# A transformer block's backward pass: attention output gradients turned in four pieces a chunk, chunk 0's q, k and v gradients kept in SBUF, a new order and new homes

## The chip, the core and the metric

The kernel runs on one core of one Trainium2 chip. The core has a matrix engine (TensorE, PE in the profile), a vector engine (VectorE, DVE), an activation engine (ScalarE, ACT), GpSimd (POOL) and a synchronisation engine (SyncE, SP), which here does nothing but issue transfers. All five run their own instruction streams in order; a transfer, once issued, is carried by 16 DMA engines. The metric is the device time of one execution in microseconds. Before the change three runs took 540.76, 541.15 and 544.3 us, median 541.15.

## What is computed

A pre-norm transformer block, forward and backward in one program, in bf16: S = 2048 rows, D = 512 columns, 32 heads of 16, F = 1792. The reference, cut to what matters:

```
q, k, v = (layernorm(x) @ wqkv) split into 32 heads of 16
idx  = pos[:, None] - 2 * arange(8)[None, :]         # window of 8 keys, 2 apart
attn = softmax(where(idx >= 0, q . k[idx] / 4, -1e9))
h    = x + (sum over the window of attn * v[idx]) @ wo
y    = h + gelu(layernorm(h) @ w1 + b1) @ w2 + b2
out, vjp = jax.vjp(block, x, wqkv, wo, w1, b1, w2, b2)
return (out, *vjp(grad_out))
```

Eight tensors come out: y and the gradients of x, wqkv, wo, w1, b1, w2 and b2.

## The kernel before, in words

The 2048 rows are worked in four chunks of 512 rows (CH). The Python functions do not issue instructions; each calls `op` (L84) to record an operation: its engine, the buffers that it reads and writes, and a function that issues its instructions. At the end `emit` (L118) walks ORDER, a table of operation numbers at the end of the file, and issues them in just that sequence. It is one sequence for all engines, so each engine's own program is what falls to it. HOMES, a second table, gives each buffer its address in SBUF (units of 64 bytes) or its PSUM bank. Two buffers may share a place if one is dead by ORDER before the other is first used, so a home can add a wait. Waits themselves are set by the framework from the buffers and addresses.

Transfers go through helpers, so in the profile they carry the helper's line: `load` L268, `store` L273, `xload` (a transfer that transposes 2-byte elements on its way) L277, `gather` L507. Nearly all are on SP's queue, where an instruction that waits holds up all that stand behind it.

The stages of a chunk, with the names that the profile uses:

- Layer norm of x (L355 to L402, tile `ln`), turned to column-major `ln1T`, for chunk 0 by TensorE (L445), for the others by a transposing transfer. Key, query and value projections (L674 with weights `wk` and `wq`, L699 with `wv`), evicted to `kt`, `qt` and `tmv` by ScalarE. While the first x is loaded, TensorE runs matmuls on a zeroed tile `wz` (L304).
- Attention scores: VectorE multiplies queries with shifted keys (`prf`, L517, 2.29 us each, four to a chunk), TensorE sums the products over a head's 16 elements (L525). Softmax, the weighted sum of values (gathered as `Ro`, `prbo` L557, L566), the output projection (L790), the residual and the second layer norm.
- Feed-forward: L826 (h times w1), gelu pieces on ScalarE (L828 `xb`, L831 `gl`), L880 (times w2, result `h2s` at L882). Feed-forward backward: L908, L910, L922, layer-norm backward L604 to L617 with results `ghr`, turned to `ghT`.
- `p3_go` (L930): the gradient of the attention's output, `got`, by L946 (`ghT` times `woT`), evicted by ScalarE in two halves. It is column-major, and the value-gradient step needs it row-major in DRAM (`go_d`), since `gather` reads bands of rows from there. `tm_dma` (L469) does that: a transposing transfer into the tile `tmgod`, then a store to `go_d`.
- `p3_dots` (L952): VectorE's products `prb` of `got` and the shifted values `vw` (L517 again), sums, softmax backward. `p3_bands` (L991): gradients of q, v and k, from gathered bands of DRAM rows (`Rq` from `k_d`, `Rv` from `go_d`, `Rk` from `q_d`), products on VectorE (`prbq`, `prbv`, `prbk`, L557), sums on TensorE (L566), evicted by ScalarE to `gqs`, `gvs` and `gks` (L571). `p3_gl1` (L1017) turns these by transposing transfers (`gqkvT`), multiplies with wqkv (L1042), and ends in layer-norm backward and the gradient of x (`gx`).
- Weight gradients, `wg_ffn` (L1083), matmuls at L1068 in groups, placed by ORDER wherever TensorE would otherwise wait, from about 200 us to the end. The last are those of wqkv, from `gqs`, `gvs`, `gks` and the layer-norm output `ln1b`.

Since the wqkv gradients come last and need all four chunks, chunk 0's `gqs`, `gvs` and `gks` are stored to DRAM (`gq_d`, `gv_d`, `gk_d`) in the kernel before and loaded again as `gq3in`; how many chunks are treated so is KEEP (L1012, L1122 to L1130). Before, KEEP is 1. `tm_dma` has two forms, chosen by `off`, the offset in the source tile, which for `got` is 0: one transposing transfer for the whole chunk, and a store whose pieces are 128 elements (256 bytes) long.

Of the kernel before, what the change touches and what calls it, by code (L numbers as in the profile page):

```python
# [148 lines left out]
def kernel(  # L149
# [319 lines left out]
    def tm_dma(fm, off, dst, c, back, tag, pm):  # L469
# [3 lines left out]
        if off:  # L473
# [609 lines left out]
    def wg_ffn():  # L1083
# [37 lines left out]
        for sel in (0, 2, 1):  # L1121
            G_ = sb("gq3in", [P, KEEP, 4, D]) if KEEP else None  # L1122
            for c in range(KEEP):
# [16 lines left out]
    for i in (1, 0, 2):  # L1140
        b = wv if i == 2 else wqk[i]
        load(b, lambda b=b: b(), lambda i=i: A_wqkv[:, i * D:(i + 1) * D].rearrange("(a p) j -> p a j", p=P), 512,
             tag="wqkv", q="ACT" if i in WQA else "SP")
# [112 lines left out]
KEEP = 1  # L1256
# [9 lines left out]
TMD = (('go', 0), ('go', 1), ('go', 2), ('go', 3))  # L1266
LNK = 0
# [179 lines left out]
```

## Time and profile before

| what | value |
|---|---|
| runs shown | 540.76, 541.15, 544.3 us |
| the profiled execution | 541.34 us, its span 539.6 us |
| TensorE busy | 524.6 us (97% of the span), 3023 matmuls |
| VectorE, ScalarE, GpSimd busy | 476.6, 335.6, 15.6 us |
| transfers | 136.61 MB, mean 253 GB/s |
| HBM | read 54.73 MB, written 37.84 MB |

The span is what the hardware profiler saw of the program; the reported time has 1.74 us around it. "Busy" counts the time that an engine executes; matmuls are pipelined, so their shown durations (379 ns) overlap, and a long run of them starts one every 0.22 us. In a row of the timeline the columns are the start, the length, the engine, the source line, the operation, what it writes and reads, the count, and in brackets the idle time before it with what ended it. "SPq" is SP's queue: the time that an issue held it, which includes waits for earlier instructions; the landing of a transfer comes later and is listed apart.

### The profile page before, as it was taken

The page shows a single profiled execution, that of the slowest core. Times are in us where ns is not written, and L with a number is a line of the kernel's source. Part 1 is how long each engine was busy: PE and PEld are TensorE (multiplying, and loading weights), DVE is VectorE, ACT ScalarE, POOL GpSimd, SP SyncE. Part 2 cuts the span into 40 slices and gives each one's busy share as a digit, 9 for nine tenths or more (in the row PEclk, how much of TensorE's full clock was granted, in tenths as well). Part 3 has the DMA queues.
Part 4 walks back from the last instruction along what each step waited for, and adds up shares of the span by engine and source line. Part 5 has one row for each costly group of instructions (what it writes and reads, how often), then busy time and mean ns, then how long its engine had stood idle before and what let it go on. Part 6 is the DMA issues. An engine that isn't in the chain of part 4 may idle for free.

```text
span 539.6 us, 8072 instructions
## 1 busy us (share of the span) xinstructions
PE 524.6 (97%) x3023; PEld 233.1 (43%) x3023; DVE 476.6 (88%) x607; ACT 335.6 (62%) x586; POOL 15.6 (3%) x23
## 2 busy tenths in 40 slices
PE   7899999999999999999999999999999999999997
PEld 3343444444444444444444444446444343443443
DVE  6889999999989999899741658999999999999993
ACT  6867859999999968977303623124343465252773
POOL 0110200000001000000000000000000000000003
PEclk9999999999999999999999999999999999999999
DMA  6999897988999999988999999999999999999977
GB/s 205 184 336 285 287 297 234 231 260 252 190 236 275 270 251 244 265 224 170 193 216 209 211 228 196 218 276 206 308 324 322 279 324 252 317 315 278 321 216 225
DMA packets 230871, 136.61 MB, mean 253 GB/s; under 512 B 188400, under 2 KB 218800, under 8 KB 226736
## 3 DMA queue, kind: packets, MB, share of 16 engines
q1 hardware_dynamic: 230448, 135.06, 98.1%
q0 software_dynamic: 384, 1.05, 0.7%
q8 instruction: 23, 0.38, 0.3%
q14 instruction: 16, 0.13, 0.1%
HBM read 54.73 MB, written 37.84 MB: 172 GB/s over the span
## 4 chain that ended last, share of the span: by engine, by line
PE 67%; DVE 14%; DMA 8%; ACT 4%; issue 3%; SPq 2%; POOL 1%; DVEq 0%; ACTq 0%
PE ps L1068 21%; PE ps L826 8%; PE ps L908 7%; PE ps L922 7%; PE ps L1042 7%; PE ps L880 6%; PE ps L566 3%; DMA Rk<-q_d 3%; DVE prf L517 3%; DVE prbk L557 3%; PE ps L946 3%; SPq L268 2%; PE ps L525 2%; DMA gqkvT<-gvs 2%; DMA v_d<-tmv 1%
## 5 line engine op out<-in xcount | busy, mean ns | idle before, releaser
L908 PE MATMUL ps<-goT,w2T 128*128 128x512 bf16 x224 | 54.1, 379 | 0.9 <-DVE h2s L882 0.8
L880 PE MATMUL ps<-w,gl 128*128 128x512 bf16 x224 | 51.3, 379 | 0.4 <-ACT gl L831 0.4
L826 PE MATMUL ps<-ln2T,w 128*128 128x512 bf16 x224 | 51.2, 379 | 0.2 <-ACT e L747 0.2
L922 PE MATMUL ps<-w1T,xb 128*128 128x512 bf16 x224 | 50.8, 379 | 0.0
L604 ACT ACTIVATE gyr<-ps,rstd 128x512 bf16<-128x512 f32 x28 | 19.0, 680 | 46.5 <-PE ps L922 31.4
L1042 PE MATMUL ps<-wqkvT,gqkvT 128*128 128x512 bf16 x192 | 44.5, 380 | 0.7 <-DMA gqkvT<-gvs 0.7
L283 ACT CAST wgs<-ps 128x512 bf16<-128x512 f32 (+1 forms) x30 | 16.4, 557 | 45.0 <-PE ps L1068 42.6
L910 DVE SCALAR_TENSOR_TENSOR xb<-xb,ps 128x512 bf16<-128x512 bf16 x56 | 37.0, 682 | 7.7 <-PE ps L908 7.4
L828 ACT ACTIVATE xb<-ps,b1c 128x512 bf16<-128x512 f32 x56 | 35.7, 693 | 7.8 <-PE ps L826 5.2
L1068 PE MATMUL ps<-gw1in,ln 128*128 128x512 bf16 (+1 forms) x192 | 39.5, 353 | 0.0
L1068 PE MATMUL ps<-gor,gw2in 128*128 128x512 bf16 x168 | 39.4, 379 | 0.0
L517 DVE TENSOR_TENSOR prf<-qt,kt 128x4096 bf16<-128x4096 bf16 x16 | 36.0, 2287 | 1.4 <-ACT qt L283 1.4
L557 DVE TENSOR_TENSOR prbv<-Rv,cfv 128x4096 bf16<-128x4096 bf16 x16 | 35.9, 2287 | 1.3 <-DMA Rv<-go_d 1.3
L557 DVE TENSOR_TENSOR prbq<-Rq,cfq 128x4096 bf16<-128x4096 bf16 x16 | 35.9, 2285 | 0.7 <-issue 0.5
L557 DVE TENSOR_TENSOR prbo<-Ro,cfo 128x4096 bf16<-128x4096 bf16 x16 | 35.8, 2287 | 0.7 <-PE ps L566 0.6
L517 DVE TENSOR_TENSOR prb<-got,vw 128x4096 bf16<-128x4096 bf16 x16 | 36.0, 2285 | 0.2
L557 DVE TENSOR_TENSOR prbk<-Rk,cfk 128x4096 bf16<-128x4096 bf16 x16 | 35.7, 2283 | 0.1
L1068 PEld LDWEIGHTS <-ln 128*128 128x128 bf16 x256 | 24.5, 98 | 25.1 <-issue 3.0
L908 PEld LDWEIGHTS <-w2T 128*128 128x128 bf16 x224 | 21.8, 98 | 27.9 <-issue 1.9
L880 PEld LDWEIGHTS <-gl 128*128 128x128 bf16 x224 | 21.5, 98 | 27.5 <-issue 1.3
L826 PEld LDWEIGHTS <-w 128*128 128x128 bf16 x224 | 21.6, 98 | 27.2 <-issue 1.8
L922 PEld LDWEIGHTS <-xb 128*128 128x128 bf16 x224 | 21.9, 98 | 26.5
(160 smaller groups left out, 921.0 us busy)
## 6 DMA issues: line engine op xcount, KB each, us to landing
Ro<-v_d SPq DMA_DIRECT2D x4, 1280.0 KB, 5.9
Rq<-k_d SPq DMA_DIRECT2D x4, 1280.0 KB, 7.6
Rv<-go_d SPq DMA_DIRECT2D x4, 1280.0 KB, 8.1
Rk<-q_d SPq DMA_DIRECT2D x4, 1280.0 KB, 7.7
g_d<-gl SPq DMA_DIRECT2D x9, 512.0 KB, 5.2
gh_d<-xb SPq DMA_DIRECT2D x9, 512.0 KB, 3.7
Ro<-v_d SPq DMA_DIRECT2D x4, 1024.0 KB, 7.8
Rq<-k_d SPq DMA_DIRECT2D x4, 1024.0 KB, 9.6
```

The source lines that it names most:

```text
L283: fn = lambda: A.copy(out=ap(), in_=pap())
L517: op("DVE", tt_us(4096), lambda g=g, pr=pr: V.tensor_tensor(out=pr(), in0=ql()[:, g, :].unsqueeze(1).to_broadcast([P, W, 512]), in1=_sub(k ...
L557: V.tensor_tensor(out=pr().rearrange("p j a (d h) -> p (j a) d h", h=H), in0=_sub(R()[:, o0, 0:1], [[1024, 4], [st, 2], [1, 512]]), in1=_s ...
L604: op("ACT", act_us(D, 1, True), lambda: A.activation(out=gyr()[:, j, :], in_=ps(), func=ACT.Copy, scale=rs[:, t:t + 1], accum_out=sg_[:, i ...
L826: T.matmul(ps(), lhsT=w1()[:, dc, f * P:(f + 1) * P], rhs=cols(ln2T[c], dc, c in FM2), start=(dc == 0), stop=(dc == DC - 1))
L828: op("ACT", act_us(512, 1), lambda f=f, ps=ps, xb=xb, f0=f0: A.activation(out=xb()[:, f - f0, :], in_=ps(), func=ACT.Identity, bias=b1c[:, ...
L880: T.matmul(ps(), lhsT=d["g"][f // 4]()[:, f % 4, j * P:(j + 1) * P], rhs=w2()[:, f, :], start=(f == 0), stop=(f == FT - 1))
L908: T.matmul(ps(), lhsT=w2T()[:, dc, f * P:(f + 1) * P], rhs=cols(goT, dc, True), start=(dc == 0), stop=(dc == DC - 1))
L910: op("DVE", 0.61, lambda f=f, ps=ps, z=z, f0=f0: V.scalar_tensor_tensor(out=z()[:, f - f0, :], in0=z()[:, f - f0, :], scalar=1.0, in1=ps() ...
L922: T.matmul(ps(), lhsT=d["d"][f // 4]()[:, f % 4, j * P:(j + 1) * P], rhs=w1T()[:, f, :], start=(f == 0), stop=(f == FT - 1))
L1042: T.matmul(ps(), lhsT=gT()[:, j, b * P:(b + 1) * P], rhs=wqkvT()[:, k0 + b, :], start=(i == 0 and b == 0), stop=(i == 2 and b == 3))
L1068: T.matmul(ps()[:, 0:N], lhsT=l, rhs=r, start=(n == 0), stop=(n == k - 1))
```

## The change

Four things change in the source; the last two are tables of numbers.

```
@@ tm_dma @@
-        if off:
+        if tag in TM4:
             for g in range(4):
                 xload(st, lambda g=g: st()[:, :, g * P:(g + 1) * P], lambda g=g: fm()[:, g, off:off + CH], 128, r=[(fm, g // 2)], key=g, tag="tmx" + tag)
             store(dst, lambda: dst()[r:r + CH, :].rearrange("(a p) d -> p a d", p=P), st, lambda: st(), 512, key=(c, 0), tag="tmst" + tag)
@@ constants @@
-KEEP = 1
+KEEP = 0
+TM4 = ('go',)
@@ tables @@
 ORDER = (
-    7, 8, 78, 10, 18, 9, 0, 6, 58, 2, 1, 11, 5, 27, 4, 21, 63, 64, 65, 59, 51, 66, 46, 42,
...
```

`got` is now turned by four transposing transfers a chunk, one for each 128 columns, of which the first two need only the first half of the eviction and the last two the second. They fill `tmgod` so that a row's 512 elements lie together, and the store to `go_d` writes rows of 1 KB. With KEEP at 0 the three stores and three loads of chunk 0's gradients are gone; the matmuls of the wqkv gradient read `gqs`, `gvs` and `gks` of chunk 0 where they lie, so these three tiles of 512 KB hold their places until the groups of their matrix are done. ORDER has 1983 operations in place of 1977, in another sequence throughout, and HOMES places the buffers anew. No engine but SP has another count of instructions; TensorE's 3023 matmuls are the same. Lines past 1267 move down by one.

Three places of the new order, before and after. First, the loads at the start on SP's queue, with `xt` the x of layer norm (`in_A_x_dram`), `wk`, `wq` and `wv` the three parts of wqkv, and `xp` x once more for the residual. Before:

```order
L268 DMA wk_5_134<-in_A_wqkv_dram 128x4x512
L268 DMA b1b<-in_B_b_dram 14x128
L268 DMA xt_13_4_131<-in_A_x_dram 32x2x1024 x3
L268 DMA xt_29_7_152<-in_A_x_dram 32x2x1024 x4
L268 DMA wq_8_185<-in_A_wqkv_dram 128x4x512
L268 DMA xp_62_9_206<-in_A_x_dram 32x2x1024
L268 DMA wv_10_208<-in_A_wqkv_dram 128x4x512
```

After:

```order
L268 DMA wk_4_126<-in_A_wqkv_dram 128x4x512
L268 DMA b1b<-in_B_b_dram 14x128
L268 DMA xt_10_3_123<-in_A_x_dram 32x2x1024 x3
L268 DMA wq_7_156<-in_A_wqkv_dram 128x4x512
L268 DMA xt_39_8_166<-in_A_x_dram 32x2x1024 x4
L268 DMA wv_9_192<-in_A_wqkv_dram 128x4x512
L268 DMA b2bc<-in_B_b_dram 128x512
```

The load of `wq` stands ahead of the four loads of chunk 2's x, and that of `wv` has no `xp` ahead of it. On TensorE, chunk 0 goes 16 key, 16 query and 16 value matmuls before, and 16 key, 12 query, 12 value, 4 query and 4 value after. Then come sums of `prf`, 8 matmuls each, among which stand groups of 8 key matmuls of chunk 1: before in the sequence sum, sum, sum, keys, sum, keys, and after sum, sum, keys, sum, sum, keys.

Second, SP's queue around the first chunks' turn of `got` (`ghT` and `gw1in`, `gw2in` are other transposes, `out_dram<-wgs` stores of weight gradients). Before:

```order
L277 DMA_TRANSPOSE gw2in_49_2928<-g_d_74 128x4x512
L277 DMA_TRANSPOSE tmgod_50_2930<-got_53_2819 128x16x128
L277 DMA_TRANSPOSE ghT_50_2936<-ghr_1183_54_2814 128x16x128
L273 DMA out_dram<-wgs_1196_55_2845 128x2x512
L273 DMA go_d<-tmgod_50_2930 512x4x128
```

After:

```order
L277 DMA_TRANSPOSE tmgod_49_2875<-got_53_2794 128x4x128
L273 DMA out_dram<-h2s_47_2644 64x1x1024
L277 DMA_TRANSPOSE wqkvT_48_2668<-in_A_wqkv_dram 128x12x128
L277 DMA_TRANSPOSE gw1in_49_2879<-gh_d_79 128x4x512
L277 DMA_TRANSPOSE tmgod_49_2875<-got_53_2794 128x4x128
L273 DMA out_dram<-wgs_1190_50_2834 128x2x512
L277 DMA_TRANSPOSE tmgod_49_2875<-got_53_2794 128x4x128 x2
L277 DMA_TRANSPOSE ghT_45_2965<-ghr_1195_50_2840 128x16x128
L277 DMA_TRANSPOSE gw2in_46_2967<-g_d_74 128x4x512
L273 DMA go_d<-tmgod_49_2875 128x4x512
```

The one transpose of a chunk is four, with other transfers between them, and the store's shape is another.

Third, VectorE around the first products of `got` (`prb`; L607, L616 and L617 are layer-norm backward, L966 the first step of softmax backward). Before:

```order
L607 ISA jk_1236_51_2941,sx<-gyr_1176_52_2802,ln_3_761_41_1883 128x512
L607 ISA sx 128x1
L617 TENSOR_TENSOR ghr_1240_51_2947<-u_1177_52_2804,gyr_1057_41_2500 128x1024
L517 TENSOR_TENSOR prb_50_2949<-got_53_2819,vw_43_2402 128x4096
L517 TENSOR_TENSOR prb_51_2951<-got_53_2819,vw_43_2402 128x4096
L617 TENSOR_TENSOR ghr_1240_51_2947<-u_1195_54_2843,gyr_1039_50_2472 128x1024
```

After:

```order
L607 ISA jk_1228_47_2921,sx<-gyr_1068_47_2508,ln_2_431_34_1161 128x512
L607 ISA sx 128x1
L517 TENSOR_TENSOR prb_47_2923<-got_53_2794,vw_48_2447 128x4096
L607 ISA jk_1230_48_2925,sx<-gyr_1065_47_2500,ln_2_431_34_1161 128x512
L607 ISA sx 128x1
L517 TENSOR_TENSOR prb_48_2928<-got_53_2794,vw_48_2447 128x4096
L616 TENSOR_TENSOR u_1207_47_2869<-u_1207_47_2869,gor_35_1889 128x1024
```

The first two products stand ahead of the L617 pair of chunk 2 (`ghr`), which was around them before.

More of the change, by code (lines that the diff above doesn't have):

```diff
@@ L472, in tm_dma @@
         r = c * CH + (RPAD if back else 0)
-        if off:
+        if tag in TM4:
             for g in range(4):
@@ L1255 @@
 LOG = None
-KEEP = 1
+KEEP = 0
 FM1 = (1, 2, 3)
@@ L1266 @@
 TMD = (('go', 0), ('go', 1), ('go', 2), ('go', 3))
+TM4 = ('go',)
 LNK = 0
```

238 rows, old and new, of tables (HOMES, ORDER) are left out of this document.

## The prediction, made before the changed kernel was run

> **What bounds the kernel now.** I read the page's busy shares first, then the clock and the DMA totals.
>
> ```profile
> PE 524.6 (97%) x3023; PEld 233.1 (43%) x3023; DVE 476.6 (88%) x607; ACT 335.6 (62%) x586; POOL 15.6 (3%) x23
> PEclk9999999999999999999999999999999999999999
> DMA packets 230871, 136.61 MB, mean 253 GB/s; under 512 B 188400, under 2 KB 218800, under 8 KB 226736
> ```
>
> TensorE is busy for 97% of the span at a clock that is never below nine tenths, and the change leaves its 3023 matmuls as they are. So the time can fall only where TensorE idles. The busy time by stretches (columns: length, then busy time of PE, weight load, DVE, ACT, POOL, clock, DMA share, GB/s) says where that is.
>
> ```profile
> 0.00:20.00 20.00, 16.35 (x75) 7.77 (x76) 13.92 (x44) 13.27 (x27) 3.24 (x10) 1.00 0.74 211
> 20.00:120.00 100.00, 95.97 (x638) 43.05 (x637) 97.30 (x102) 82.52 (x136) 5.58 (x3) 1.00 0.97 266
> 120.00:160.00 40.00, 40.00 (x209) 17.58 (x207) 37.26 (x62) 38.98 (x55) 1.01 (x1) 1.00 0.92 229
> 160.00:200.00 40.00, 38.65 (x178) 17.24 (x177) 39.37 (x65) 37.11 (x48) 1.43 (x1) 1.00 1.03 271
> 200.00:260.00 60.00, 60.00 (x279) 27.20 (x278) 56.98 (x113) 48.37 (x80) 0.00 (x0) 1.00 0.91 218
> 260.00:320.00 60.00, 60.00 (x279) 27.20 (x278) 26.85 (x65) 19.00 (x43) 0.00 (x0) 1.00 1.13 210
> 320.00:400.00 80.00, 80.00 (x540) 37.74 (x539) 76.93 (x54) 25.18 (x54) 0.00 (x0) 1.00 1.06 248
> 400.00:500.00 100.00, 97.95 (x633) 40.09 (x632) 98.24 (x64) 44.89 (x93) 0.00 (x0) 1.00 1.04 302
> 500.00:520.00 20.00, 20.00 (x133) 8.38 (x132) 19.82 (x27) 16.96 (x36) 0.00 (x0) 1.00 0.97 279
> 520.00:540.00 20.00, 15.63 (x73) 6.85 (x71) 9.98 (x20) 9.38 (x21) 4.35 (x8) 0.99 0.76 223
> ```
>
> Length less PE busy: 3.65 us idle in the head, 4.03 in 20 to 120, 1.35 in 160 to 200, 2.05 in 400 to 500, 4.37 in the tail, and none in 120 to 160, 200 to 400 and 500 to 520. That is 15.45 us, of which 7.43 lie between head and tail. One per cent is 5.4 us: to gain that, nearly all of the 7.43 would have to go. Note also DVE: 33.15 us idle from 260 to 320, then 194.99 busy of 200 from 320 to 520.
>
> The profiled execution was reported at 541.34 us, 1.74 beyond its span of 539.6, and the median of the runs shown is 541.15. I sum from 541.3 and take 0.2 off at the end.
>
> **The gradient turned in four pieces, and its store.**
>
> ```profile
> L277 SPq DMA_TRANSPOSE tmgod<-got x4: 2377/3162/5197, 311.5 to 446.4; - x4
> L277 SPq DMA_TRANSPOSE gw2in<-g_d x12: 1226/2290/3505, 183.0 to 327.5; - x12
> go_d<-tmgod SPq DMA_DIRECT2D x4, 512.0 KB, 4.4
> k_d<-ftk SPq DMA_DIRECT2D x4, 512.0 KB, 3.1
> q_d<-ftq SPq DMA_DIRECT2D x4, 512.0 KB, 4.4
> L557 DVE TENSOR_TENSOR prbv<-Rv,cfv 128x4096 bf16<-128x4096 bf16 x16 | 35.9, 2287 | 1.3 <-DMA Rv<-go_d 1.3
> ```
>
> One transpose of a whole chunk holds SP's queue for 2.38 us at the least (first row). A piece of a quarter is not in the trace. Below it lies a quarter of 2.38, 0.6; above it the least of a transpose of the same size class, 1.23 (second row, 512 KB of g_d, so larger). I take 0.8: four pieces hold the queue 3.2 us, 0.8 more per chunk (0 to +2.5), 3.3 us over four chunks. What stands behind them are weight-gradient stores, other transposes and the gathers of k; the cover is TensorE's run without idle from 200 to 400, and without that cover it would cost those 3.3 us (up to 10). The store in 1 KB rows is the form of the fourth and fifth rows: 3.1 to 4.4 us to landing against 4.4. The only reader is the gather Rv, and DVE waited for it 1.3 us in all (last row). So the store is worth 0 to 1.3, and that is part of the stretch 400 to 500 below.
>
> A sentence that the sum doesn't need: the Trainium skill, "DMA: Bandwidth & Descriptors", section "Rules for kernel authors", says that many small transfers should be coalesced into one large one, which speaks against four transposes of 128 KB in place of one of 512 KB. By it the sum's part for the turn would go up, not down; no row here shows a quarter piece.
>
> **Chunk 0's gradients kept in SBUF.**
>
> ```profile
> gq3in<-gq_d SPq DMA_DIRECT2D x1, 512.0 KB, 10.4
> gk_d<-gks SPq DMA_DIRECT2D x1, 512.0 KB, 11.3
> 494.61 3.18 SPq L277 DMA_TRANSPOSE gqkvT<-gks  x1
> 497.84 0.58 SPq L507 DMA_DIRECT2D Rk<-q_d  x1
> 498.46 0.43 SPq L268 DMA_DIRECT2D gq3in<-gk_d  x1
> 498.93 0.43 SPq L507 DMA_DIRECT2D Rk<-q_d  x1
> ```
>
> Three stores and three loads of 512 KB go: 3.1 of 136.61 MB, 12.4 us of traffic at the mean 253 GB/s, and six issues of some 0.43 to 0.58 us, one of them between two gathers (the last three rows, SP's queue: start, length). They fall where the DMA share stands at 1.04, and took up to 11.3 us to land (the first two rows), so the gathers and transposes of 400 to 500 beside them may land earlier. The matmuls that read the reloaded tile read the kept one instead, at the same cost.
>
> **The order from 260 to 500.**
>
> ```profile
> 316.58 0.69 DVE L617 TENSOR_TENSOR ghr<-u,gyr 128x1024 bf16<-128x1024 bf16 x1 [6.43 <-PE ps L1068]
> 317.19 4.49 DVE L517 TENSOR_TENSOR prb<-got,vw 128x4096 bf16<-128x4096 bf16 x2
> 414.69 0.61 PE L566 MATMUL ps<-prbq,S 128*32 128x512 bf16 x8 [0.62 <-DVE prbq L557]
> 495.65 1.90 PE L1042 MATMUL ps<-wqkvT,gqkvT 128*128 128x512 bf16 x8 [0.74 <-DMA gqkvT<-gvs]
> ```
>
> The first product of the attention backward starts at 317.19, right after DVE idled 6.43 us for an operation of layer-norm backward (L617). In the new order it stands ahead of that pair, so DVE's long run may begin up to 6.4 us earlier. But it is ahead of nothing on TensorE, which has no idle until 400. It pays only in the waits that TensorE has for DVE and DMA in 400 to 500, such as the last two rows. I take half of their 2.05 as gone with the DMA relief: -1.0 (-2.05 to +3.3, the upper end if all of the longer SP time comes through). What is late next is then the gathers.
>
> **The head.**
>
> ```profile
> 1.96 6.46 PE L304 MATMUL ps<-wz 128*128 128x512 bf16 x17 [1.96 <-DVE wz L299]
> 10.30 3.61 PE L674 MATMUL ps<-ln1T,wk 128*128 128x512 bf16 x16 [0.75 <-ACT ln1T L283]
> 14.78 3.65 PE L674 MATMUL ps<-ln1T,wq 128*128 128x512 bf16 x16 [0.87 <-DMA wq<-in_A_wqkv_dram]
> 24.61 0.61 PE L525 MATMUL ps<-prf,S 128*32 128x512 bf16 x8 [0.88 <-DVE prf L517]
> 25.69 1.92 PE L674 MATMUL ps<-ln1T,wk 128*128 128x512 bf16 x8 [0.47 <-DMA ln1T<-ln]
> 28.08 1.92 PE L674 MATMUL ps<-ln1T,wk 128*128 128x512 bf16 x8
> 4.58 4.41 SPq L268 DMA_DIRECT2D xt<-in_A_x_dram  x7
> 9.03 0.59 SPq L268 DMA_DIRECT2D wq<-in_A_wqkv_dram  x1
> 17.78 2.29 DVE L517 TENSOR_TENSOR prf<-qt,kt 128x4096 bf16<-128x4096 bf16 x1 [1.40 <-ACT qt L283]
> 19.90 3.52 SPq L277 DMA_TRANSPOSE ln1T<-ln  x1
> 525.97 9.66 PE L1068 MATMUL ps<-gks,ln1b 128*128 128x512 bf16 x44
> ```
>
> Seven loads take 4.41 us to issue, 0.63 each. The load of wq now goes ahead of four of them, so it lands 2.5 us earlier and the wait of 0.87 ends. Its queries come up to 0.87 earlier, and with them the first product (prf, which idled 1.40 for them), unless it then waits for statistics of chunk 2, whose x comes 0.63 later. Against that, TensorE now does chunk 1's first eight key matmuls after the second sum of prf and no longer after the third. The second sum ended at 23.73 (24.61 less the wait of 0.88) and may end at 22.9; the ln1T of chunk 1, whose transpose was issued at 19.90 behind the queries' copies, let TensorE on at 25.69, and may at 24.8. So one wait of 1.9 stands where 0.88 and 0.47 stood. Behind it come those eight keys (8 times 0.22, which is 9.66 over 44 in the last row), two sums of 0.61 and eight more keys, done 4.7 us after ln1T: 29.5, against 30.0 before (28.08 and 1.92). If ln1T comes no earlier, it is 30.4. I take -0.5, near the first, since the copies ahead of ln1T do come earlier (bounds: -1.2, if ln1T gains the queue's time too; +1.1, if it comes 0.8 later than before).
>
> On the clock, in sentences by themselves: the Trainium skill, "TensorE: Matmul & The Clock Gate", section "What's actually happening", puts the clock at half after an idle window of about 3.4 us. The first 17 warm-up matmuls took 6.46 us, 0.38 each, so a slow start is in this trace, but no idle stretch of that length once they are done. A wait for ln1T that grew to that would cost 2.7 us more by that row (6.46 less 17 times 0.22).
>
> **The rest.** 20 to 120, past the head's waits: 2.7 us of idle in many pieces under 1 us, all in another order now; nothing there is tied to the edits, so 0 (-1.5 to +1.5). 160 to 200: gelu pieces on ScalarE and gradient pieces on VectorE now stand earlier against the matmuls that need them; half of 1.35, -0.7 (-1.35 to +1.5). Tail: the same matmuls last (the run of gks, above) and the same stores, with one group of four later than before: 0 (0 to +0.9). 120 to 160 and 200 to 400: nothing to gain, and cover.
>
> Sum: 541.3 - 0.5 - 1.0 - 0.7 = 539.1; less 0.2 for the median, 538.9 us.
>
> **The rivals.** *Nothing comes of it* (540 to 542): the gaps only change place. For: none of the edits lies where TensorE idles for more than 2.05 us. Against: the wait for wq has a plain cure. 541.0. *Nearly all idle goes* (under 535.7): DVE's run starts 6 us earlier, the gathers are never late, and 20 to 120 is tighter. 541.3 - 0.2 - 1.2 - 1.5 - 1.35 - 2.05 = 535.0. For: the waits shown are all under 1 us after the start, so each has a small cause. Against: no single edit reaches 20 to 120. *SP's queue becomes the bound* (slower): a piece of the turn waits for its half of an eviction, with the gather Rq of the first bands behind it in the same queue. If pieces cost 1.23, SP loses 2.5 us a chunk, 10 in all. DVE has 5 us idle in 320 to 520 (200 less 194.99); once the delay of its gathers is past that, TensorE waits one for one: from 5 us on. With 10 it is 5, and with the waits in front of each of the four chunks (the largest so far 0.74) 3 more: 541.3 - 0.2 + 8 - 0.5 = 548.6. For: DVE is busy for 97% there. Against: the pieces are issued earlier than the whole was, and each waits for half of the gradient, not for all. *A small loss* (542 to 546.6): the head's ln1T wait or a new gap in 20 to 200, at most +1.1 and +3.0 by the bounds: about 544. *The clock falls* in the head: 541.3 + 1.1 + 2.7 = 545.1, only if a wait in the head triples.
>
> **How the numbers follow.** Forecast (537 to 540) 0.42; nothing 0.20; nearly all idle gone 0.15; SP's queue 0.10; small loss 0.11; clock 0.02. A measurement of this kernel can tell about one per cent from no change. Faster by over 1% (under 535.7) is the third, 0.15; slower by over 1% (above 546.6) is the fourth, 0.10; within, 0.75. Range: below, 534.5, which holds the 535.0 of the third case with 0.5 for its unknown pieces; above, 545.5, for the small loss and the clock, which leaves out SP's queue.
>
> **What would show it.** Right: no wait of wq's first matmul for its load; a first prf near 16.9; a first prb before 314; gaps in 400 to 500 summing to about 1 us; DMA bytes near 133.5 MB; TensorE still busy about 524 us. Wrong: TensorE idle in 200 to 400, which was all cover; DVE waits for Rq or Rv of over 2 us; a stretch of the clock below 1.00 after the head; or a wait over 2.5 us in the first 30 us.

## The result, and the profile after

The changed kernel takes 537.24 us (median of 7 runs, 536.42 to 540.05) against 542.26 for the kernel before (7 runs): a ratio of 0.9912, 95% interval 0.9888 to 0.9936. A second set of runs (experiment 5) gave 537.82 against 541.52, 0.9933 (0.992 to 0.9945). The ratios are of fast runs alone: one run of the kernel before, of 782.8 us, and one of experiment 3, of 1106.98 us, are in the medians that are given and not in the ratios. So the change saves 3.7 to 5 us, under one per cent. The profiled execution took 536.42 us with a span of 534.5, 4.9 and 5.1 less than before. The forecast was 538.9, a gain of 2.2 from the median then known.

From the page of the changed kernel:

```profile
PE 518.0 (97%) x2975; PEld 234.4 (44%) x3023; DVE 475.7 (89%) x607; ACT 335.4 (63%) x586; POOL 17.0 (3%) x23
DMA packets 224247, 133.47 MB, mean 250 GB/s; under 512 B 180496, under 2 KB 212944, under 8 KB 220112
```

The bytes fell from 136.61 to 133.47 MB, the six transfers of chunk 0. TensorE's row shows 2975 matmuls, but 3023 weight loads: 48 matmul records are missing from this trace, so its busy time reads too low and the idle time too high. One experiment below (`g_wq_back`: the changed kernel with one load of the head put back, the same time within the noise) has all 3023 records. I read TensorE from that one. Its page:

```profile
PE 521.4 (97%) x3023; PEld 234.7 (44%) x3023; DVE 475.9 (89%) x607; ACT 335.4 (63%) x586; POOL 17.0 (3%) x23
```

and its stretches (columns as in the prediction):

```profile
20.00:120.00 100.00, 93.95 (x634) 42.65 (x633) 97.17 (x100) 82.05 (x134) 5.30 (x4) 1.00 0.97 268
...
160.00:200.00 40.00, 39.96 (x186) 18.02 (x185) 39.25 (x62) 35.70 (x47) 1.11 (x1) 1.00 0.94 248
...
400.00:500.00 100.00, 99.94 (x666) 42.63 (x665) 99.66 (x64) 47.62 (x99) 0.00 (x0) 1.00 1.00 299
```

Idle time, length less busy time of TensorE, went from 2.05 us to 0.06 from 400 to 500 and from 1.35 to 0.04 from 160 to 200, while from 20 to 120 it grew from 4.03 to 6.05. And TensorE is busy 521.4 us for the same 3023 matmuls, 3.2 less than before. The prediction had said that it would stay near 524.

The head of the changed kernel on TensorE, then on VectorE:

```profile
1.18 5.65 PE L304 MATMUL ps<-wz 128*128 128x512 bf16 x13 [1.18 <-DVE epsc L314]
...
12.96 2.75 PE L674 MATMUL ps<-ln1T,wq 128*128 128x512 bf16 x12
...
22.59 0.62 PE L525 MATMUL ps<-prf,S 128*32 128x512 bf16 x8 [1.15 <-DVE prf L517]
24.32 1.92 PE L674 MATMUL ps<-ln1T,wk 128*128 128x512 bf16 x8 [1.12 <-DMA ln1T<-ln]
...
29.30 0.59 PE L744 MATMUL ps<-mx,nident 128*128 128x512 bf16 x2
```

```profile
16.98 2.28 DVE L517 TENSOR_TENSOR prf<-qt,kt 128x4096 bf16<-128x4096 bf16 x1
20.17 0.16 DVE L393 SCALAR_TENSOR_TENSOR rstd<-mv,rstd 128x4 f32<-128x4 f32 x1 [0.90 <-POOL rstd L390]
20.25 6.69 DVE L517 TENSOR_TENSOR prf<-qt,kt 128x4096 bf16<-128x4096 bf16 x3
```

The query matmuls no longer wait for `wq`, and the first `prf` starts at 16.98. The two waits that follow, 1.15 and 1.12, are those of before in another shape. One part of the first is new: VectorE stops 0.90 us for the statistics of chunk 2 that GpSimd finishes, between the first `prf` and the second. In the kernel before, the second `prf` follows the first (17.78) without a stop, and so it starts earlier than here. That row, on VectorE, and the end of the head, on TensorE, are

```profile
20.06 6.69 DVE L517 TENSOR_TENSOR prf<-qt,kt 128x4096 bf16<-128x4096 bf16 x3
...
29.84 0.59 PE L744 MATMUL ps<-mx,nident 128*128 128x512 bf16 x2
```

so the head is worth 0.54 us in this execution. The other traces with the same head do not show that gain (experiment 5).

The turn on SP's queue and the first products of `got` in the changed kernel (the tile views: shortest, median and longest time in ns, first and last start in us):

```profile
L277 SPq DMA_TRANSPOSE tmgod<-got x16: 1189/1267/2540, 298.4 to 418.4; - x16
L517 DVE TENSOR_TENSOR prb<-got,vw x16: 2282/2286/2293, 306.1 to 379.3; 128x4096 bf16<-128x4096 bf16 x16
```

A piece of a quarter holds the queue for 1.27 us, and never under 1.19. Four are 5.1 us against 3.16 for the whole. `prb` starts at 306.1, 11 us earlier than before. And TensorE's last run of 44, which began at 525.97:

```profile
519.90 9.66 PE L1068 MATMUL ps<-gks,ln1b 128*128 128x512 bf16 x44
```

It begins 6.07 us earlier. The span is only 5.1 shorter: from the last copy out of PSUM to the end of the span it takes 4.3 us in place of 3.4, with the last stores.

**Where the gain on TensorE came from.** A matmul's shown length overlaps the next, so short waits are hidden in the busy time. I therefore counted the times from one matmul's start to the next start in the traces of before and `g_wq_back`, both complete. Where nothing is late these are the same everywhere: 0.216 us from one full matmul to the next, 0.309 from a full one to the first of a run of sums (the matmuls of 32 columns, L525 and L566), and from the first sum of a run to the next full one 0.548 us for a run of 8 sums, 0.979 for 16, 1.411 for 24, 1.842 for 32. Each further 8 sums are 0.432, so a run of sums costs 0.116 beyond its sums, and 0.093 on the way in (0.309 less 0.216): **0.209 us for each run, however long**. The kernel before has 43 such runs, the changed one 34, with the same 96 groups of 8 sums. A run of 8 in the kernel before:

```profile
372.43 0.62 PE L566 MATMUL ps<-prbq,S 128*32 128x512 bf16 x8
372.97 1.48 PE L1068 MATMUL ps<-gw1in,ln 128*128 128x256 bf16 x12
```

Whatever exceeds these intervals I call a wait.

| from the first matmul's start, us | before | `g_wq_back` | difference |
|---|---|---|---|
| waits, first 20 us | 4.82 | 4.33 | -0.49 |
| waits, 20 to 120 | 6.25 | 7.35 | +1.10 |
| waits, 120 to 200 | 1.83 | 0.69 | -1.14 |
| waits, 200 to the end | 2.93 | 0.58 | -2.35 |
| runs of sums, 0.209 each | 43 | 34 | -1.88 |
| sum | | | -4.76 |
| first start to last start | 533.28 | 528.47 | -4.81 |

The sum must close but for rounding, since a wait is by definition what the intervals do not explain; what the table adds is where the time went. The row of the first 20 us is that of a kernel with `wq` put back. Before the first matmul another 0.78 is gained (1.96 against 1.18), and at the end 1 to 2 us is lost. The trace of the changed kernel itself gives -5.28 from first to last start, with the same 34 runs.

### The profile page after: what moved, and what is told of

The parts are those of the page before. It is cut to its first block, busy times and chain, and to the rows that moved or that the text cites. A ratio compares the mean times of both kernels' runs of the same rounds, so it can differ in the third digit from the quotient of the medians.

```text
span 534.5 us, 8044 instructions
## 1 busy us (share of the span) xinstructions
PE 518.0 (97%) x2975; PEld 234.4 (44%) x3023; DVE 475.7 (89%) x607; ACT 335.4 (63%) x586; POOL 17.0 (3%) x23
## 2 busy tenths in 40 slices
DMA packets 224247, 133.47 MB, mean 250 GB/s; under 512 B 180496, under 2 KB 212944, under 8 KB 220112
## 4 chain that ended last, share of the span: by engine, by line
PE 70%; DVE 14%; ACT 5%; issue 4%; DMA 3%; SPq 2%; POOL 1%; DVEq 0%; ACTq 0%
PE ps L1068 23%; PE ps L922 9%; PE ps L908 8%; PE ps L1042 7%; PE ps L880 7%; PE ps L826 6%; DVE prbo L557 5%; PE ps L566 4%; PE ps L946 3%; DVE prf L517 2%; DMA Rk<-q_d 2%; ACT xb L828 1%; PE ps L525 1%; POOL rstd L390 1%; DVE st L375 1%
## 5 line engine op out<-in xcount | busy, mean ns | idle before, releaser
L1042 PE MATMUL ps<-wqkvT,gqkvT 128*128 128x512 bf16 x185 | 42.6, 379 | 0.8 <-issue 0.6
L1068 PE MATMUL ps<-gor,gw2in 128*128 128x512 bf16 x164 | 38.0, 379 | 0.5 <-issue 0.3
L880 PEld LDWEIGHTS <-gl 128*128 128x128 bf16 x224 | 21.6, 98 | 27.9 <-ACT mv L368 1.5
L826 PEld LDWEIGHTS <-w 128*128 128x128 bf16 x224 | 21.6, 98 | 27.8 <-issue 2.9
```

What stands on the lines that cost most here:

```text
L826: T.matmul(ps(), lhsT=w1()[:, dc, f * P:(f + 1) * P], rhs=cols(ln2T[c], dc, c in FM2), start=(dc == 0), stop=(dc == DC - 1))
L880: T.matmul(ps(), lhsT=d["g"][f // 4]()[:, f % 4, j * P:(j + 1) * P], rhs=w2()[:, f, :], start=(f == 0), stop=(f == FT - 1))
L1042: T.matmul(ps(), lhsT=gT()[:, j, b * P:(b + 1) * P], rhs=wqkvT()[:, k0 + b, :], start=(i == 0 and b == 0), stop=(i == 2 and b == 3))
L1068: T.matmul(ps()[:, 0:N], lhsT=l, rhs=r, start=(n == 0), stop=(n == k - 1))
```

## The experiments

Each variant has ORDER and HOMES of its own where needed; the edit is given against the kernel named in its heading, with rows of an engine's order where ORDER is edited. None leaves out any of the computation. "The old order" is ORDER of the kernel before, with as few homes moved as the edit needs.

**1. The turn in four pieces alone, old order** (against the kernel before; the four pieces stand where the one turn stood).

```
-        if off:
+        if tag in TM4:
+TM4 = ('go',)
-L277 DMA_TRANSPOSE tmgod_50_2930<-got_53_2819 128x16x128
+L277 DMA_TRANSPOSE tmgod_50_2930<-got_53_2819 128x4x128 x4
```

> The kernel before, its order and homes kept, with the turn of the attention output gradient in four pieces and the 1 KB store alone (each of the four transposes stands where the one stood; chunk 0's gradients are still stored and reloaded). Theory (the order makes the gain: fewer changes between sums and other matmuls on TensorE, fillers in the waits, an earlier start): ratio to before 0.998 to 1.003, TensorE's waits in 400 to 500 within 0.5 us of before's 2. Rival (the edits make it, by relief of the queue and the DMA engines): ratio 0.993 to 0.997, the waits in 400 to 500 halved. Second rival (four pieces hold SP's queue longer): ratio above 1.003.

546.17 us against 540.7, ratio 1.0104 (1.008 to 1.0128): slower by 5.5 us. On SP's queue, first of this variant:

```profile
339.14 5.79 SPq L277 DMA_TRANSPOSE tmgod<-got  x4
...
355.45 6.07 SPq L277 DMA_TRANSPOSE tmgod<-got  x4
...
374.28 1.07 SPq L273 DMA_DIRECT2D out_dram<-wgs  x2
```

and of the kernel before:

```profile
351.73 3.03 SPq L277 DMA_TRANSPOSE tmgod<-got  x1
...
370.57 1.04 SPq L273 DMA_DIRECT2D out_dram<-wgs  x2
```

Four pieces in a row hold the queue for 6 us where the whole held it for 3, and two stores of weight gradients behind them go out at 374.28 in place of 370.57. Who waits for those is seen on ScalarE and TensorE of the variant:

```profile
379.41 0.37 ACT L283 CAST wgs<-ps 128x256 bf16<-128x256 f32 x1 [8.21 <-DMA out_dram<-wgs]
```

```profile
379.83 1.49 PE L566 MATMUL ps<-prbq,S 128*32 128x512 bf16 x24 [3.02 <-ACT wgs L283]
```

ScalarE cannot overwrite the staging tile `wgs` until its store has landed, the sums wait for that copy, and TensorE loses 3.02 us where it lost none in the kernel before:

```profile
375.42 1.49 PE L566 MATMUL ps<-prbq,S 128*32 128x512 bf16 x24
```

That is 3 of the 5.5 us. The theory that pieces are hidden falls. The rival with SP's queue holds in the old order, but its price is paid through a store, not through the gather Rq that the rival had named.

**2. The changed kernel with the turn in one piece** (against the changed kernel; the one stands at the place of the last of the four).

```
-TM4 = ('go',)
+TM4 = ()
```

> The changed kernel with the turn put back to one transpose a chunk and 256-byte store pieces, the one transpose standing where the last of the four stood; order, homes and kept gradients otherwise as in the changed kernel. Theory (the order makes the gain): ratio to before 0.990 to 0.993, as the changed kernel's 0.991, with TensorE idle within 1 us of the changed kernel. Rival (the edits make it): 0.994 to 0.998, with waits for the gather of the gradient rows back in 400 to 500.

537.98 us, 0.9957 (0.9938 to 0.9975) against 0.9912 and 0.9933 with four pieces: a difference of 1 to 2 us, near what the intervals can tell. Its one new wait is

```profile
453.20 1.04 PE L1042 MATMUL ps<-wqkvT,gqkvT 128*128 128x512 bf16 x4 [0.93 <-DMA gqkvT<-gqs]
```

In the new order the pieces stand apart (second place in the part on the change), and there they cost nothing; whether they gain 1 to 2 us these runs do not settle. The holds of SP's queue fit that. In the new order the four whole turns hold it 20.4 us in all (2.9 to 7.8 each, in this variant), the sixteen pieces 22.0. In the old order it was 13.9 for the whole turns and 21.6 for the pieces.

**3. The changed kernel with the stores and loads of chunk 0, the loads issued shortly before their use** (against the changed kernel; one of the three places on SP's queue).

```
-KEEP = 0
+KEEP = 1
+L268 DMA gq3in_41_4056<-gq_d 128x2048
+L273 DMA gk_d<-gks_45_3951 128x2048
 L507 DMA Rk_40_4110<-q_d 128x5120
```

> The changed kernel with chunk 0's q, k and v gradients stored to DRAM and loaded again (six transfers of 512 KB back, put at about the places that they had before; the reloaded tile takes the place of the stored one). Theory (the order makes the gain): ratio to before 0.990 to 0.994, at most 1 us of new waits in 400 to 500. Rival (the edits make it): 0.994 to 0.998, with 2 us of waits in 400 to 500 as before.

549.98 us, 1.0165 (1.0141 to 1.0189). SP's queue, then TensorE:

```profile
435.25 5.73 SPq L277 DMA_TRANSPOSE gqkvT<-gks  x1
441.03 0.58 SPq L268 DMA_DIRECT2D gq3in<-gq_d  x1
```

```profile
446.73 1.04 PE L1068 MATMUL ps<-gq3in,ln1b 128*128 128x512 bf16 x4 [3.62 <-DMA gq3in<-gq_d]
...
512.59 1.79 PE L1068 MATMUL ps<-gq3in,ln1b 128*128 128x512 bf16 x4 [3.64 <-DMA gq3in<-gk_d]
```

The load stands behind a transpose that holds the queue 5.73 us, and its reader starts 5.1 us after the load's issue ended. The two waits of 3.6 us come from where I placed the loads more than from having them; experiment 6 places them earlier.

**4. The new order alone: KEEP = 1 and one piece, loads placed as in 3** (against the changed kernel).

```
-KEEP = 0
+KEEP = 1
-TM4 = ('go',)
+TM4 = ()
```

> The new order and homes alone: one transpose a chunk with 256-byte store pieces, and chunk 0's gradients stored and loaded again, both as before the change. Theory (the order makes the gain): ratio to before 0.990 to 0.995, with 34 changes of TensorE from other matmuls to sums as in the changed kernel and waits of under 0.5 us in 160 to 200. Rival (the edits make it): 0.997 to 1.003.

555.48 us, 1.0275 (1.0251 to 1.0299), with a wait of

```profile
450.34 1.89 PE L1068 MATMUL ps<-gq3in,ln1b 128*128 128x512 bf16 x4 [7.74 <-DMA gq3in<-gq_d]
```

The theory that the order by itself makes the gain is not borne out, but the late loads are in this number, and the order alone with early loads was not run. Experiment 3 differs from this one in the pieces alone, and is faster by 1.1 per cent: here the one transpose of `got` at 421.86 holds SP's queue 7.63 us, and the wait for the load that comes later is 7.74 in place of 3.62. So with late loads the pieces gain.

**5. The changed kernel again**, beside the next three.

> The changed kernel once more, unaltered, on the same chip as the next three, to compare them with it. Ratio to before 0.988 to 0.994 if the first measurement holds.

537.82 us, 0.9933 (0.992 to 0.9945). Its head does not run as in the first trace: TensorE waits for `wv`, the first `prf` starts at 18.0 in place of 17.0 and L744 at 30.30 in place of 29.30.

```profile
16.73 2.75 PE L699 MATMUL ps<-wv,ln1T 128*128 128x512 bf16 x12 [1.06 <-DMA wv<-in_A_wqkv_dram]
```

The order of the head is the same in experiments 2, 3, 4, 6 and 7. Their traces have L744 at 30.82, 30.97, 31.15, 31.65 and 30.81. The four traces of the old order (the kernel before, experiments 1, 8 and 9) have it at 29.57 to 29.84. So six of seven traces show the new head later than the old one, by about 1 us in the middle, and the first trace's gain of 0.54 is the exception.

**6. As 3, with the loads 25 to 60 us ahead of their use** (against experiment 3, SP's queue).

```
+L268 DMA gq3in_44_3916<-gq_d 128x2048
 L268 DMA xr_43_3854<-in_A_x_dram 32x2x1024
...
-L268 DMA gq3in_41_4056<-gq_d 128x2048
...
+L268 DMA gq3in_41_4123<-gv_d 128x2048
```

> The changed kernel with chunk 0's q, k and v gradients stored and loaded again, now with each of the three loads issued 25 to 60 us ahead of its first matmul and into the place of the stored tile. Theory A (in the first version the reloads were merely issued too late, 441.0 for a use at about 441): the two waits of 3.8 us are gone, 0 to 2 us above the changed kernel on this chip. Theory B (six more transfers of 512 KB hold back the gathers and transposes around them, wherever they stand): 4 us or more above the changed kernel, with waits on gathers or turned gradients in 400 to 500.

544.88 us, 1.0065 (1.005 to 1.0081), 7.1 us above experiment 5. No matmul waits for a reloaded tile now. What waits instead, on SP's queue, VectorE and TensorE:

```profile
446.79 9.66 SPq L277 DMA_TRANSPOSE gqkvT<-gqs  x1
```

```profile
420.48 2.29 DVE L557 TENSOR_TENSOR prbk<-Rk,cfk 128x4096 bf16<-128x4096 bf16 x1 [3.28 <-DMA Rk<-q_d]
```

```profile
459.93 1.89 PE L1042 MATMUL ps<-wqkvT,gqkvT 128*128 128x512 bf16 x4 [3.68 <-DMA gqkvT<-gqs]
461.61 1.91 PE L1068 MATMUL ps<-gqs,ln1b 128*128 128x512 bf16 x4
463.46 2.99 PE L566 MATMUL ps<-prbk,S 128*32 128x512 bf16 x32
```

The gather Rk is 3.28 us late, the transposed gradient 3.68, and after that idle stretch the next matmuls start 0.42 to 0.46 us apart (461.61 less 459.93, over 4), half of full speed. This execution took 548.03 us, the longest of the six, so that stretch need not be in the others. In the new order, then, keeping chunk 0 in SBUF is worth about 7 us, by the queue, the gathers and the waits that follow, and not by fewer matmuls.

**7. The changed kernel with its runs of sums divided**: 68 runs in place of 34, each group of 8 sums issued apart from the next where other matmuls could be put between (against the changed kernel, TensorE, one place).

```
-L566 MATMUL ps<-prbv,S x32
+L566 MATMUL ps<-prbv,S x8
+L1068 MATMUL ps<-gw1in,ln x4
+L566 MATMUL ps<-prbv,S x8
+L1068 MATMUL ps<-gw1in,ln x4
+L566 MATMUL ps<-prbv,S x8
+L1068 MATMUL ps<-ghr,ro x4
+L566 MATMUL ps<-prbv,S x8
```

> The changed kernel with 34 more changes of TensorE between the 128x32 sums and other matmuls: in the attention backward a weight-gradient or gx group of four that followed a run of sums is put between two sums of the run (68 runs of sums and not 34); the work is the same. Theory (each change costs 0.21 us, from the intervals in both traces: a run of 8 sums takes 548 ns, 8 more 432, and the matmul ahead of a run 309 in place of 216): 6 to 9 us above the changed kernel on this chip, shared out over all the changes, no wait over 1.5 us. Rival (the changes are free, and only waits for DVE and DMA count): within 1.5 us of the changed kernel, or all of the loss in a few waits of DVE's buffers.

557.45 us, 1.0304 (1.0288 to 1.0319). One piece of the changed kernel, and one of the variant:

```profile
445.46 1.91 PE L566 MATMUL ps<-prbq,S 128*32 128x512 bf16 x32
447.31 3.63 PE L1068 MATMUL ps<-gqs,ln1b 128*128 128x512 bf16 x15
```

```profile
388.29 0.61 PE L525 MATMUL ps<-prb,S 128*32 128x512 bf16 x8
388.83 1.04 PE L1068 MATMUL ps<-gw1in,ln 128*128 128x512 bf16 x4
389.80 0.61 PE L525 MATMUL ps<-prb,S 128*32 128x512 bf16 x8
```

In the variant eight sums and four full matmuls take 1.51 us (389.80 less 388.29). Inside longer runs it would be 0.43 for the sums and 0.86 for four of 0.216, 1.30 in all: 0.21 less. The 32 sums of the changed kernel (447.31 less 445.46) take 1.85, and pay it once. From first to last matmul it takes 18.9 us longer than experiment 5; by the same count, waits are 11.4 of these, which leaves 7.5. The 34 further runs at 0.209 are 7.1. That the two are close follows from how a wait is counted and is no proof; what bears the price out is that the same intervals stand at the new places: 56 of the 68 runs begin 0.309 us after the full matmul ahead of them, and of the 51 runs of 8, 40 take 0.548 to the next full one. The total of 19.6 us is over the 6 to 9 expected, and near 371 there is a wait of 1.97 us for ScalarE's copy of `got`, where none over 1.5 was expected. TensorE waits for other copies too (`gqs` 2.9 us in all), and VectorE's busy time from 320 to 400 falls from 74.66 to 67.52 us. That sums which come later hold VectorE's product buffers longer would fit this, but is only argued. Runs of sums cannot be priced by their changes alone.

**8. Chunk 0 kept in SBUF alone, old order**, one piece, 26 buffers with other homes (against the kernel before).

```
-KEEP = 1
+KEEP = 0
```

> The kernel before, its order kept, with chunk 0's gradients kept in SBUF alone (six transfers fewer; the one transpose and the 256-byte store pieces as before). The three tiles of 512 KB hold their places longer, so 26 buffers of the attention backward and later have other homes. Theory (the gain needs the new order, since it is fewer changes and better fillers on TensorE): ratio to before 0.997 to 1.006. Rival (the six transfers were what held the end back): 0.990 to 0.996, with the waits of 400 to 500 (2 us) gone.

543.08 us against 541.52, 1.0031 (1.0016 to 1.0047). Six transfers less, and no gain. The trace has a wait that the kernel before had not:

```profile
476.70 0.61 PE L566 MATMUL ps<-prbq,S 128*32 128x512 bf16 x8 [1.36 <-DVE prbq L557]
```

The three kept tiles take room, and the buffers that had to move may be freed later; that is not shown. I did not separate the homes from the missing transfers.

**9. Both edits in the old order** (against the kernel before).

```
-        if off:
+        if tag in TM4:
-KEEP = 1
+KEEP = 0
+TM4 = ('go',)
```

> The kernel before, its order kept, with both edits: the turn in four pieces at the place of the one, and chunk 0's gradients kept in SBUF (26 buffers with other homes, as in the run of the kept gradients alone). The two edits alone gave 1.0104 and 1.0031. Theory (the edits gain nothing without the new order, since four pieces in a row hold SP's queue ahead of the gather Rq): ratio to before 1.005 to 1.014, and TensorE's wait of about 3 us for prbq near 375 again. Rival (the freed queue makes up for the longer turn): 0.995 to 1.002.

550.58 us, 1.0192 (1.0155 to 1.0229), more than the two alone add up to (1.0135). SP's queue and TensorE:

```profile
355.20 5.48 SPq L277 DMA_TRANSPOSE tmgod<-got  x4
```

```profile
379.77 2.75 PE L566 MATMUL ps<-prbq,S 128*32 128x512 bf16 x24 [3.94 <-ACT wgs L283]
```

The wait of experiment 1 again, 0.9 us longer, and this time the 24 sums behind it take 2.75 us where they took 1.49: half speed.

**10. The changed kernel with `wq` loaded behind the four loads of x, as before** (against the changed kernel, SP's queue).

```
-L268 DMA wq_7_156<-in_A_wqkv_dram 128x4x512
-L268 DMA xt_39_8_166<-in_A_x_dram 32x2x1024 x4
+L268 DMA xt_38_7_164<-in_A_x_dram 32x2x1024 x4
+L268 DMA wq_8_190<-in_A_wqkv_dram 128x4x512
```

> The changed kernel with one transfer moved back: the load of wq stands behind the four loads of chunk 2's x again, as before the change. Theory (the load's place is what took the wait for wq away): TensorE waits 0.7 to 1.5 us at its first matmul with wq, and the first submax matmul (L744) starts 0.3 to 1.0 us later than in the changed kernel; time 0 to 1 us above it, hardly to be told by times. Rival (wq lands in time anyway, or the wait is only moved to wv): L744 starts at the same time within 0.2 us.

537.82 us, 0.9941 (0.9918 to 0.9964), not to be told from the changed kernel. A wait for `wq` comes back, shorter than the 0.87 of before and than the theory's 0.7 to 1.5:

```profile
13.51 2.78 PE L674 MATMUL ps<-ln1T,wq 128*128 128x512 bf16 x12 [0.41 <-DMA wq<-in_A_wqkv_dram]
```

L744 starts at 29.56, between the two executions of the changed kernel (29.30 and 30.30) and earlier than in six of the seven traces with `wq` in its new place. The place of `wq`, on which the prediction's head rested, is worth nothing that can be measured.

**11. Another head**: `wv` two loads earlier, the second `prf` ahead of the statistics that VectorE had waited 0.90 us for, and chunk 2's normalised rows later on ScalarE (against the changed kernel, VectorE and ScalarE).

```
 L517 TENSOR_TENSOR prf_15_294<-qt_84_13_250,kt_59_10_200 128x4096
+L517 TENSOR_TENSOR prf_16_308<-qt_84_13_250,kt_59_10_200 128x4096
 L393 SCALAR_TENSOR_TENSOR rstd<-mv,rstd 128x4
...
-L398 ACTIVATE ln_2_109_15_305<-xt_39_8_166,rstd 128x512
-L283 CAST tmv_16_307<-ps 128x1024
-L398 ACTIVATE ln_2_109_15_305<-xt_39_8_166,rstd 128x512 x3
+L283 CAST tmv_15_304<-ps 128x1024
+L398 ACTIVATE ln_2_120_16_345<-xt_39_8_166,rstd 128x512 x4
```

> An attempt at a better version: the changed kernel with four moves in the head. VectorE does the second product prf ahead of the small operation that waits 0.9 us for GpSimd; ScalarE normalises chunk 2 behind the values' copy; TensorE does the third sum of prf ahead of chunk 1's keys, in its wait for ln1T; the load of wv goes ahead of two of chunk 2's x loads. Theory (each of the waits of 0.9 to 1.3 us seen in the head is worth what it lasts, until the next): the first L744 starts 0.6 to 1.5 us earlier than in the changed kernel, the time falls by as much. Rival (VectorE or the landing of ln1T sets the pace there): under 0.3 us.

539.15 us, 0.9962 (0.9935 to 0.9989): no better. L744 starts at 31.41; in the traces without these moves it was at 29.30 to 31.65. The first sums come no earlier, since TensorE now waits for ScalarE ahead of them:

```profile
22.20 1.02 PE L304 MATMUL ps<-wz 128*128 128x512 bf16 x4 [2.12 <-ACT tmv L283]
...
26.71 0.62 PE L525 MATMUL ps<-prf,S 128*32 128x512 bf16 x8 [1.66 <-DVE prf L517]
```

**12. As 11, with the load of w2 (tile `w`, 1792 KB) ahead of the transpose `oT`**, to end the wait of 1.04 us for it near 93 us (against experiment 11, SP's queue).

```
-L277 DMA_TRANSPOSE oT_344_26_939<-ost_27_875 128x16x128
-L268 DMA w_351_33_957<-in_B_w_dram 128x14x512
+L268 DMA w_344_26_939<-in_B_w_dram 128x14x512
+L277 DMA_TRANSPOSE oT_345_27_941<-ost_27_875 128x16x128
```

> The version before this one, and besides the load of w2 (1.8 MB) issued ahead of the transpose oT of chunk 2, up to 5 us earlier than the 86.5 of the changed kernel. Theory: TensorE's wait of 1.1 to 1.3 us for it at the first feed-forward output goes, 1 us below the version before this one. Rival (its traffic then holds back oT, whose reader already waited 0.8 us): no gain, the wait for oT over 1.5 us.

545.45 us, 1.0086 (1.0054 to 1.0117): 6.3 us worse than experiment 11. SP's queue and TensorE:

```profile
83.96 0.39 SPq L268 DMA_DIRECT2D w<-in_B_w_dram  x1
85.27 8.86 SPq L277 DMA_TRANSPOSE oT<-ost  x1
```

```profile
96.16 5.17 PE L790 MATMUL ps<-wo,oT 128*128 128x512 bf16 x16 [5.41 <-DMA oT<-ost]
```

The transpose holds the queue 8.86 us where it was 4.31 in experiment 11 and 3.06 in the changed kernel, and TensorE waits 5.41 for it, then starts at a lower speed (16 matmuls in 5.17 us). No variant that I tried beats the changed kernel.

**The experiments together.**

| | neither edit | four pieces | chunk 0 kept | both |
|---|---|---|---|---|
| old order | 1 | 1.0104 | 1.0031 | 1.0192 |
| new order | 1.0275 (late loads) | 1.0165 (late loads), 1.0065 (early loads) | 0.9957 | 0.9912, 0.9933 |

In the old order each edit costs time, and the two together more. In the new order the gain needs chunk 0 kept: with it the kernel is faster with one piece (0.9957) as with four, and without it all three runs are slower. The pieces cost 5.5 us in the old order and nothing that can be told in the new one. So edits and order act together, and neither can be priced without the other. The traces suggest that they meet in SP's queue; what the order is worth by itself, with early loads, stays open.

## Why the prediction was right and where it was wrong

The time lies inside the range, on the side that was forecast and within one per cent, as the likeliest case had it. The gain was 1.7 to 2.2 times the 2.2 us forecast, and several terms came out for reasons other than those given. Part of the nearness is luck: a saving of 1.9 us, the fewer runs of sums, was not in the sum; the head, which was, went the other way in most traces; and a loss at the end that was put at nothing took 1 to 2 us off.

- **That with the same 3023 matmuls the time can fall only where TensorE idles.** This step failed. The same matmuls in another sequence take 1.9 us less, since 34 runs of sums in place of 43 save nine changes at 0.209 us. The rows for it lay in the kernel before: the runs of 8, 16, 24 and 32 sums are in its timeline. The order of TensorE shows how many runs there are, and I had not counted them. The Trainium skill, "TensorEngine Tiling (Array Packing)", section "Key Properties", says that a change of tiling mode drains TensorE; it gives no figure, and 0.209 us for the two changes around a run is what these traces put beside it.
- **400 to 500, -1.0.** The idle time of 2.05 us went entirely. The mechanism, relief of SP's queue, is supported in the new order by experiment 6 (7 us with the six transfers back). In the old order the same relief gained nothing (experiment 8), so it does not work by itself. Mis-sized by half.
- **160 to 200, -0.7.** Half of 1.35 was taken; all of it went (1.31 in the windows). No experiment isolates why.
- **20 to 120, 0.** Idle grew by 2.0 us in the windows (1.1 in waits counted from start to start). It lay inside the bounds of ±1.5 only by the second count. This is where part of the gain was given back.
- **The head, -0.5.** Wrong in sign in most traces. Against 29.84 for the kernel before, L744 starts 0.54 us earlier in one of seven traces with this head and 0.46 to 1.81 later in the other six; the middle one is 0.98 later, near the upper bound of +1.1. The wait for `wq` ended as said, but its place is worth nothing measurable (experiment 10), and the first `prf` came near 16.9 only in the first trace (16.98; else 17.30 to 18.19). In all seven, VectorE starts the second `prf` 3.3 us after the first, where it was 2.3 in the old order, since the statistics of chunk 2 stand between them. The prediction had named that condition for the first `prf`, and put it at nothing for the second. Experiment 11 moved that stop away and L744 came no earlier, so that it is the whole loss is not shown.
- **Four pieces at 0.8 us more a chunk.** It is 1.9 in the old order (four of 1.27 less 3.16), and 0.4 in the new one, where the whole turn too holds the queue longer (experiment 2): the row to go by was the least of the larger transposes, 1.23, and not a quarter of 2.38. A part of the price doesn't shrink with the size. That agrees with the rule to coalesce that the prediction took from the Trainium skill, and in the old order the rule decides: 5.5 us slower. In the new order it does not, and the measurement decides: four pieces are no slower than one.
- **The rival with SP's queue, 548.6.** As a mechanism it was real: experiments 1 and 9 measured 546.2 and 550.6. In the changed kernel, where the pieces stand apart and the six transfers are gone, it did not come. It had named the gather Rq where the traces have the stores of `wgs`.
- **The tail, 0 (0 to +0.9).** It was +1.0, and 1.9 in `g_wq_back`. Not explained.

Of the signs listed at the end, `prb` before 314 (306.1), bytes of 133.5 MB and no wait of VectorE for gathers over 2 us came true; a first `prf` near 16.9 did in one trace of seven; TensorE busy about 524 did not.

## What to carry to other kernels

When the order of an engine's work changes, count the changes of kind along it as well as the instructions: where two kinds of matmul alternate, gathering the smaller kind into longer runs saves a fixed time for each run, as long as no product buffer is held for it. Before an edit that splits or removes a transfer is priced by its own time, look at what stands behind it in its queue, and at the copies and buffers which those wait for. And when a change has several parts, test them in the old order and in the new one: here the parts alone mislead. A head that differs by up to 2.3 us from one execution to the next needs several traces before a gain of half a microsecond is read from it.

## What the runs showed of the hardware that was not expected

**Some transposing transfers held SP's queue until earlier transfers had landed.** From the kernel before, and from experiment 5:

```profile
359.21 7.55 SPq L277 DMA_TRANSPOSE vw<-v_d  x1
```

```profile
438.56 7.97 SPq L277 DMA_TRANSPOSE gqkvT<-gqs  x1
...
461.35 9.58 SPq L277 DMA_TRANSPOSE gqkvT<-gqs  x1
```

Of the transfers issued ahead of each of the three, the last to land did so 7.83, 8.08 and 9.75 us after the transpose's own start, 0.1 to 0.3 us after the hold ended. In experiment 12 it was 8.86 against 9.10, with `w` the transfer ahead; in experiment 11, where that load stood behind the transpose, the hold was 4.31. Over the 83 transposes of the kernel before that had something under way, the hold ended 0.13 us ahead of that landing in the median, half of the differences lay within about 0.4 us of nothing, and the correlation of the two lengths was 0.77. That is inferred from the landings that the trace has, and not a law: three pieces of `got` in experiment 5 held the queue for 1.23 to 1.27 us with 5.0 to 6.4 still to go. What decides between the two is open. If it holds, a large transfer just ahead of a transpose costs SP the transfer's whole time, and six transfers of 512 KB can be worth 7 us; that last link was argued from these rows and not tried by itself.

**Half speed after an idle stretch.** After waits of 2.12 us (experiment 11) and 3.02 (experiment 1) TensorE went on at full speed; after 3.22 (experiment 4), 3.64, 3.68, 3.94, 5.41 and 7.74 us the next matmuls came at about half speed, 0.43 us apart, for 3.3 to 5.9 us. After one wait of 3.62 (experiment 3) the first six came at full speed and the next at half; the granted clock there is 0.50 from 447.9 to 451.3. The Trainium skill, "TensorE: Matmul & The Clock Gate", section "What's actually happening", puts the limit at an idle window of about 3.4 us; the traces agree roughly, with full speed after 3.02 and half after 3.22.
